# A gated mix of attention and feed-forward: the last gate factor applied earlier, and the last fill in two halves

## The chip, the cores and the metric

The kernel runs on one core of one Trainium2 chip. The metric is the device time of one execution in microseconds (us). In the profile PE is TensorE's matmuls, PEld its weight loads, DVE is VectorE, ACT ScalarE, POOL GpSimd and SP SyncE, which here only issues DMAs.

## The reference

With x of 2048 rows and 640 columns, out = g*a + (1-g)*b, where g = sigmoid(x . gate_w) is one number per row:

```python
g = _sigmoid((x * gate_w).sum(-1, keepdims=True))
a = _A_ref(x, A_wq, A_wk, A_wv, A_wo, A_beta)   # causal attention in 4 chunks of 512 rows, 32 heads of 20,
                                                # mixed with a running linear memory, then o @ wo
b = (silu(x @ w1) * (x @ w3)) @ w2              # feed-forward, 1728 inner columns
return g * a + (1 - g) * b
```

## The kernel before, in words

Everything is held transposed: 640 features are 5 blocks of 128 partitions, and the 2048 rows are 4 chunks (c = 0 to 3) of 512 columns. Chunks are worked in pairs, A = (0, 1) and B = (2, 3). Every fp32 factor of a large matmul is split into a high and a low part and multiplied in three passes (`PASSES`: high x high, weight's low x high, weight's high x low), so one projection of a block of 128 outputs over 640 inputs is 15 matmuls of 128x128 weights against 512 columns (`proj`).

The 1728 inner columns of the feed-forward are 14 units j (13 of 128, and j = 13 of 64), in five groups, the last of which is `[13, 12]`. `ffn_up(cs, j, ...)` computes for each chunk the gate product `pg`, then with ScalarE's tanh `t` and VectorE `u = (t+1)*pg`, then the product `pu`, then `t = u*0.5*pu`, and splits it into `ht` (high part by ScalarE, low part by GpSimd, line 107). For j = 13 gate and up products come out of one set of 15 matmuls, in the lower and the upper 64 partitions. `ffn_down(cs, js, ...)` multiplies the units of a group by w2: for each chunk and each of 5 feature blocks fb one PSUM bank, a fill, which VectorE adds to the sums `accs[c]`. The attention's output projection `oproj(c, ...)` adds to the same sums: its first part, `normalize`, divides the head outputs by their sums, adds the memory's read and splits the result; its second part is 5 fills of 15 matmuls (line 784), each added by VectorE.

The factor 1-g of a chunk, `shares[c]`, is one number per row, stored in DRAM and loaded by `load_share(c)` over all partitions (256 KB, from ScalarE's queue). (The attention's part is scaled by g/(1-g) in advance.) Chunk 0 gets it in its last down fills, chunk 1 in its output projection, and chunks 2 and 3 in their last down fills: `finish` adds the fill to the sum (line 515), multiplies by the share (line 516, by VectorE or, for even fb, by GpSimd) and stores the block from SP's queue (line 517). The very last block is added, multiplied and stored in two halves of 256 columns.

Weights come through `w_load` (SP's queue, into one of two raw buffers) and `w_split`: GpSimd casts the tile to its high part (line 174) and subtracts for the low part (line 175) into one of six W tiles; a raw buffer is free again after the low part, and a W tile after TensorE's last use. `w_get` asks for a tile; `w_step`, called at every step of the program that yields no float, loads and splits ahead.

PSUM banks (`bank_tile`) are taken in turn from a list of eight.

TensorE's order is the program's own: generators yield after a few matmuls, and `chain`, `braid` and `weave` mix them (`braid(a, b, every)` takes a step of b after each `every` steps of a). The order on the other engines is set by a planner with modelled costs, except where `here` keeps the program's order; each engine then works off its own list in that order. The end of the program, after the attention, is `tail`: the down fills of group 3, then units 13 and 12 for chunks 2 and 3, braided with `normalize(3)`; then the output projection of chunk 3; then the last down fills, 10 of them with 5 matmuls each.

## Time and profile before

| | us |
|---|---|
| three runs | 1109.91, 1107.6, 1111.63 (median 1109.91) |
| the profiled execution | 1109.41 |
| its span, first to last instruction | 1107.7 |
| PE busy | 1094.4 (99%) |
| DVE, POOL, ACT busy | 592.6 (53%), 584.7 (53%), 381.2 (34%) |

The profile is of one execution. A row of a timeline has the start, the duration, engine, line, operation, what is written and read with its shape, and in brackets the engine's idle time before it and who ended it. A row marked x2 or more merges neighbours: the duration is from the first start to the last end. SPq and ACTq rows are the issue of a DMA alone. The ends of matmuls are modelled. The granted TensorE clock is 1.000 of full speed.

### The profile page before, as it was taken

How to read it: one execution, taken by the hardware profiler on the slowest of the kernel's cores; microseconds unless marked ns; L12 is line 12 of the kernel's file. 1: busy time of each engine (PE TensorE's matmuls, PEld its weight loads, DVE VectorE, ACT ScalarE, POOL GpSimd, SP SyncE). 2: the span in 40 equal slices, each digit the busy share in tenths (PEclk: the TensorE clock that was granted, in tenths of full speed). 3: DMA queues.
4: the chain of work that ended last, by engine and by line, in shares of the span. 5: the costliest groups of instructions: out<-in, count | busy, mean ns of one | idle time of the engine just before them, and what ended most of it. 6: DMA issues, size and time to landing. Idle time of an engine off the chain costs nothing.

```text
span 1107.7 us, 17867 instructions
## 1 busy us (share of the span) xinstructions
PE 1094.4 (99%) x6285; PEld 852.9 (77%) x6285; DVE 592.6 (53%) x1708; ACT 381.2 (34%) x826; POOL 584.7 (53%) x729
## 2 busy tenths in 40 slices
PE   9999999999999999999999999999999999999997
PEld 6988877777777777788977777777777777777786
DVE  5032564356555554366154678875557765551645
ACT  6244233343233122145244543424343332233120
POOL 5055556366366363565175547555764556565253
PEclk9999999999999999999999999999999999999999
DMA  9266943334165132636268967455654433432122
GB/s 327 89 205 220 282 123 82 95 82 125 46 165 127 53 82 93 156 95 196 95 203 269 288 203 193 104 156 144 162 136 113 108 96 94 113 103 87 51 79 95
DMA packets 87545, 153.20 MB, mean 138 GB/s; under 512 B 11584, under 2 KB 25184, under 8 KB 87456
## 3 DMA queue, kind: packets, MB, share of 16 engines
q1 hardware_dynamic: 63040, 106.30, 30.4%
q0 software_dynamic: 20384, 38.68, 15.8%
q10 hardware_dynamic: 4032, 7.08, 1.8%
q8 instruction: 50, 0.82, 0.3%
q14 instruction: 39, 0.32, 0.1%
HBM read 96.56 MB, written 54.54 MB: 136 GB/s over the span
## 4 chain that ended last, share of the span: by engine, by line
PE 91%; DVE 4%; DMA 1%; ACT 1%; issue 1%; POOL 1%; SPq 0%; ACTq 0%; DVEq 0%; POOLq 0%
PE f L534 16%; PE g L253 16%; PE u L253 15%; PE v L364 6%; PE k L253 6%; PE op L784 6%; PE o L634 6%; PE q L253 6%; PE s L581 5%; PE t L614 4%; PE nd L331 1%; PE pm L428 1%; DVE junk L588 1%; PE pkt L413 1%; PE gt L713 1%
## 5 line engine op out<-in xcount | busy, mean ns | idle before, releaser
L588 DVE CUSTOM_DVE_ANT_0 junk<-s,mask 128x256 bf16<-128x256 f32 (+3 forms) x512 | 250.5, 489 | 106.3 <-PE s L581 74.1
L620 ACT ACTIVATE P<-t 128x512 f32<-128x512 f32 (+1 forms) x384 | 172.5, 536 | 192.1 <-PE t L614 154.8
L253 PE MATMUL g<-X,W 128*128 128x512 f32 x840 | 208.7, 398 | 0.0
L175 POOL TENSOR_TENSOR W<-wr,W 128x640 fp32r<-128x640 f32 (+1 forms) x126 | 200.3, 1596 | 2.3
L174 POOL CAST W<-wr 128x640 fp32r<-128x640 f32 (+1 forms) x126 | 91.0, 726 | 207.5 <-PE f L534 46.9
L534 PE MATMUL f<-ht,W 128*128 128x512 f32 x820 | 196.6, 397 | 0.3 <-POOL W L175 0.3
L253 PE MATMUL u<-X,W 128*128 128x512 f32 x780 | 196.7, 399 | 0.0
L624 POOL TENSOR_SCALAR_AFFINE_SELECT P<-P 128x256 f32<-128x256 f32 x192 | 94.6, 501 | 180.8 <-ACT P L620 180.6
L253 PEld LDWEIGHTS g<-X,W 128*128 128x128 f32 x840 | 155.9, 188 | 36.7 <-issue 0.4
L534 PEld LDWEIGHTS f<-ht,W 128*128 128x128 f32 x820 | 152.7, 188 | 37.0 <-POOL W L175 0.8
L253 PEld LDWEIGHTS u<-X,W 128*128 128x128 f32 x780 | 144.0, 188 | 34.5 <-ACT P L620 0.3
L107 POOL TENSOR_TENSOR ht<-ft,ht 128x512 fp32r<-128x512 f32 x52 | 67.1, 1291 | 91.3 <-ACT ht L106 90.8
L558 POOL DMA_DIRECT2D qk<-qkd x128 | 83.5, 654 | 0.3
L581 PE MATMUL s<-qk 60*128 60x256 f32 (+3 forms) x512 | 78.2, 345 | 2.2 <-DVE m L588 1.0
L253 PE MATMUL k<-X,W 128*128 128x512 f32 x300 | 77.0, 403 | 0.0
L634 PE MATMUL o<-P,vg 128*32 128x512 f32 (+3 forms) x1024 | 75.5, 435 | 1.4 <-DVE on L714 1.4
L253 PE MATMUL q<-X,W 128*128 128x512 f32 x300 | 74.0, 400 | 1.3 <-DVE X L107 0.7
L493 ACT ACTIVATE ft<-g 128x512 f32<-128x512 f32 x52 | 31.2, 599 | 125.7 <-PE g L253 114.7
L494 DVE SCALAR_TENSOR_TENSOR fu<-ft,g 128x512 f32<-128x512 f32 x52 | 35.7, 686 | 68.1 <-ACT ft L493 59.1
L364 PE MATMUL v<-W,X 128*128 128x320 f32 (+1 forms) x480 | 71.6, 311 | 0.3 <-ACT P L620 0.3
L364 PEld LDWEIGHTS v<-W,X 128*128 128x128 f32 x480 | 71.0, 189 | 0.8 <-ACT P L620 0.6
L106 ACT CAST ht<-ft 128x512 fp32r<-128x512 f32 x52 | 32.2, 619 | 111.9 <-DVE ft L500 111.8
(118 smaller groups left out, 1170.1 us busy)
## 6 DMA issues: line engine op xcount, KB each, us to landing
qk<-qkd POOLq DMA_DIRECT2D x128, 240.0 KB, 4.2
wr<-in_w_dram SPq DMA_DIRECT2D x80, 320.0 KB
qkd<-qs SPq DMA_DIRECT2D x20, 512.0 KB
qkd<-ks SPq DMA_DIRECT2D x20, 512.0 KB
od<-oq SPq DMA_DIRECT2D x32, 256.0 KB
wr<-in_wo_dram SPq DMA_DIRECT2D x20, 320.0 KB
vg<-vd SPq DMA_DIRECT2D x16, 336.0 KB
xr<-in_xT_dram SPq DMA_DIRECT2D x20, 256.0 KB
```

Source lines behind the costliest of these rows:

```text
L107: (lo or nc.gpsimd.tensor_sub)(dst[:, 1], src, dst[:, 0].bitcast(F32))
L174: nc.gpsimd.tensor_copy(w[:, 0, :n], raw[:, :n])
L175: nc.gpsimd.tensor_sub(w[:, 1, :n], raw[:, :n], w[:, 0, :n].bitcast(F32))
L253: nc.tensor.matmul(ps, w[:, a, kb * P:(kb + 1) * P], x[:, b, kb, :], start=n == 0, stop=n == 14)
L364: nc.tensor.matmul(ps[:, :n1 - n0], x[:, a, kb, lb * P:(lb + 1) * P], wvt[kb][:, b, n0:n1], start=n == 0, stop=n == 14)
L534: nc.tensor.matmul(ps, w, h, start=n == 0, stop=n == len(ms) - 1)
L558: here(nc.gpsimd.dma_start(t[64 * i:64 * i + RH], qkd[c][RH * (h + i):RH * (h + i + 1)]))
L581: nc.tensor.matmul(ps[i][:, o:o + w], q[:, qb * P:(qb + 1) * P], key[:, :w], start=n == 0, stop=n == len(todo) - 1, skip_group_check=True)
L588: nc.vector.tensor_tensor_reduce(out=junk[:, :w], in0=ps[i][:, o:o + w], in1=mask[:, L - w:], scale=1.0, scalar=-3.0e38, op0=ALU.add, op1= ...
L620: last["exp"] = nc.scalar.activation(pairs[2 * m + k]["P"][:, i, o:o + n], ps[i][:, b:b + n], AF.Exp, scale=SCALE)
L624: nc.gpsimd.affine_select(d, d, pattern=[[0, 2], [0, n], [1, P]], base=0, channel_multiplier=-1, compare_op=ALU.is_ge, fill=0.0)
L634: nc.tensor.matmul(ps[32 * i:32 * i + 32, kb * P:], heads[2 * p + i]["v"][:, kb], pairs[p + i // 2]["P"][:, i % 2, o:o + n], start=kb == 0 ...
```

## The change

For chunks 2 and 3 the factor 1-g no longer comes behind the last fills. It goes into the addends instead:

- `ffn_up` for the units of the last group multiplies `u` by the share (VectorE), so the last fills come out scaled.
- The sums so far are scaled before the last fills: those of chunk 3 right after the output projection's add, by VectorE; those of chunk 2 by GpSimd, in five steps braided into the output projection of chunk 3 (`shared(2)`).
- The last fills are then only added and stored (`finish_shared`).
- The two shares are loaded after the down fills of group 3 (`both_shares`), ahead of units 13 and 12; that of chunk 3 takes the slot of the head outputs `oq` in place of one of the four `f` tiles.
- The last fill of chunk 3 is made in two halves of 256 columns, each in a bank of its own.

The new generators add seven steps to the program, so `normalize`'s last step is braided 6 matmuls earlier, ahead of unit 13, and `w_step` is called seven times more.

```diff
     def ffn_up(cs, j, idx, oldest=None):
         half = j == NF
+        shares_in = cs == B and j in GROUPS[-1]
...
                 nc.vector.scalar_tensor_tensor(u, t, 1.0, pg, op0=ALU.add, op1=ALU.mult)
+                if shares_in:
+                    nc.vector.tensor_mul(u, u, shares[c])
...
                 nc.vector.scalar_tensor_tensor(u[:64], t[:64], 1.0, pg[:64], op0=ALU.add, op1=ALU.mult)
+                if shares_in:
+                    nc.vector.tensor_mul(u[:64], u[:64], shares[c][:64])
...
-    def finish(c, fb, ps, end=False):
-        dst = accs[c][:, fb]
-        for n0 in ((0, 256) if end else (0,)):
-            d, p, g = (t[:, n0:n0 + (256 if end else L)] for t in (dst, ps, shares[c]))
-            nc.vector.tensor_add(d, p, d)
-            (nc.gpsimd if c and fb % 2 == 0 and not end else nc.vector).tensor_mul(d, d, g)
-            nc.sync.dma_start(out[c, fb, :, n0:n0 + d.shape[-1]], d)
+    def share(c, fb):
+        d = accs[c][:, fb]
+        (nc.gpsimd if c == 2 or c == 1 and fb % 2 == 0 else nc.vector).tensor_mul(d, d, shares[c])
+
+    def finish(c, fb, ps):
+        d = accs[c][:, fb]
+        nc.vector.tensor_add(d, ps, d)
+        share(c, fb)
+        nc.sync.dma_start(out[c, fb], d)
+
+    def finish_shared(c, fb, ps, n0, n):
+        d = accs[c][:, fb, n0:n0 + n]
+        nc.vector.tensor_add(d, ps[:, :n], d)
+        nc.sync.dma_start(out[c, fb, :, n0:n0 + n], d)
+
+    def shared(c):
+        for fb in range(KB):
+            share(c, fb)
+            yield 1
...
-            if c in last:
+            if c in last and c < 2:
                 load_share(c)
...
+                for n0, n1 in ((0, 256), (256, L)) if last and (c, fb) == (NSEG - 1, KB - 1) else ((0, L),):
...
+                        nc.tensor.matmul(ps[:, :n1 - n0], w, h, start=n == 0, stop=n == len(ms) - 1)
...
+                    elif c < 2:
+                        finish(c, fb, ps)
+                    else:
+                        finish_shared(c, fb, ps, n0, n1 - n0)
+    def both_shares():
+        for c in B:
+            load_share(c)
+            yield 1
...
-        shares[c] = f_tile("sh") if c == NSEG - 1 else sp.tile([P, L], F32, tag="share", name=f"sh{c}", bufs=1)
+        shares[c] = sp.tile([P, L], F32, tag="oq" if c == NSEG - 1 else "share", name=f"sh{c}", bufs=1)
...
                     nc.vector.tensor_add(dst, ps, dst)
+                    if c == NSEG - 1:
+                        share(c, fb)
...
-    tail = [braid(chain([d] + u), o1, 4, 10)] + [o2, job_down(B, 4, B)]
+    tail = [braid(chain([d, (0, both_shares())] + u), o1, 4, 10)] + [braid(o2, (0, shared(2)), 3), job_down(B, 4, B)]
```

The planner's order on GpSimd for the end of the program, before and after (wo1 to wo5 are the output projection's weight tiles in their order of use, w2h and w2 those of units 13 and 12, "ht" the low part of unit 12, x share the multiplies by the share):

```
before: cast wo1, cast wo2, low wo1, low wo2, cast wo3, cast wo4, low wo3, low wo4, ht chunk 2,
        cast wo5, low wo5, cast w2h, ht chunk 3, low w2h, cast w2, low w2, 5 x share (chunks 2 and 3)
after:  cast wo1, cast wo2, low wo1, 5 x share (chunk 2), low wo2, cast wo3, cast wo4, low wo3, ht chunk 2,
        low wo4, cast wo5, ht chunk 3, cast w2h, low wo5, low w2h, cast w2, low w2
```

On TensorE, VectorE, ScalarE and SP the orders of the two kernels are alike up to `normalize(3)`, apart from names.

More of the change, by code (lines that the diff above doesn't have):

```diff
@@ L527, in ffn_down @@
             for fb in range(KB):
-                ps = bank_tile(f"f{c}_{js[0]}_{fb}", 1300 if len(js) > 2 else 690)
-                ms = []
-                for j, w in zip(js, w2s):
-                    for a, b in (PASSES if j < NF else ((0, 0), (0, 1))):
-                        ms.append((w[:, b, fb * P:(fb + 1) * P], hts[c, j][:, a, :]))
-                for n, (w, h) in enumerate(ms):
-                    nc.tensor.matmul(ps, w, h, start=n == 0, stop=n == len(ms) - 1)
-                    if n % 3 == 2 and n < len(ms) - 1:
-                        yield 699.0 if n == 2 and len(ms) > 5 else 699
-                filled()
-                dst = accs[c][:, fb]
-                if first:
-                    nc.scalar.copy(dst, ps)
-                elif c not in last:
-                    nc.vector.tensor_add(dst, ps, dst)
-                else:
-                    finish(c, fb, ps, (c, fb) == (NSEG - 1, KB - 1))
-                yield 699 if len(ms) % 3 == 0 else 466
+                for n0, n1 in ((0, 256), (256, L)) if last and (c, fb) == (NSEG - 1, KB - 1) else ((0, L),):
+                    ps = bank_tile(f"f{c}_{js[0]}_{fb}_{n0}", 1300 if len(js) > 2 else 690)
+                    ms = []
+                    for j, w in zip(js, w2s):
+                        for a, b in (PASSES if j < NF else ((0, 0), (0, 1))):
+                            ms.append((w[:, b, fb * P:(fb + 1) * P], hts[c, j][:, a, n0:n1]))
+                    for n, (w, h) in enumerate(ms):
+                        nc.tensor.matmul(ps[:, :n1 - n0], w, h, start=n == 0, stop=n == len(ms) - 1)
+                        if n % 3 == 2 and n < len(ms) - 1:
+                            yield 699.0 if n == 2 and len(ms) > 5 else 699
+                    filled()
+                    dst = accs[c][:, fb]
+                    if first:
+                        nc.scalar.copy(dst, ps)
+                    elif c not in last:
+                        nc.vector.tensor_add(dst, ps, dst)
+                    elif c < 2:
+                        finish(c, fb, ps)
+                    else:
+                        finish_shared(c, fb, ps, n0, n1 - n0)
+                    yield 699 if len(ms) % 3 == 0 else 466
+    def both_shares():
+        for c in B:
+            load_share(c)
+            yield 1
     oall, heads, pairs = {}, {}, {}
```

## The prediction

> **What bounds the kernel now.** The page comes first, then the chain of waits over the last 40 us, then the timelines of that stretch engine by engine.

> ```profile
> PE 1094.4 (99%) x6285; PEld 852.9 (77%) x6285; DVE 592.6 (53%) x1708; ACT 381.2 (34%) x826; POOL 584.7 (53%) x729
> ```

> TensorE (PE) is busy 99% of the span, 1094.4 of 1107.7 us. Time can be won where it has nothing more to do, and is lost wherever it is made to wait. The instruction streams of the two kernels as built differ in this last stretch alone (normalize of chunk 3, units 13 and 12, the output projection of chunk 3, last fill), so the sum concerns these 60 us. The chain there:

> ```profile
> 1069.50 3.50 PE u L253 x15
> 1073.00 17.50 PE op L784 x75
> 1090.50 8.08 PE f L534 x35
> ...
> 1101.83 1.27 DVE acc L516
> 1103.10 0.67 DVE acc L515 x2
> 1103.77 0.33 DVE acc L516
> 1104.10 0.34 DVEq L1020
> ```

> TensorE carries it through 75 matmuls of the projection (17.50/75 = 0.233 each) into the last fills; then VectorE takes over. The timelines of the end:

> ```profile
> 1090.34 11.70 PE L534 MATMUL f<-ht,W 128*128 128x512 f32 x50
> ...
> 1093.57 0.73 DVE L516 TENSOR_TENSOR acc<-acc,sh 128x512 f32<-128x512 f32 x1
> ...
> 1101.28 1.28 POOL L516 TENSOR_TENSOR acc<-acc,sh 128x512 f32<-128x512 f32 x1 [1.23 <-DVE acc L515]
> 1101.83 1.27 DVE L516 TENSOR_TENSOR acc<-acc,sh 128x512 f32<-128x512 f32 x1
> 1103.02 0.74 DVE L515 TENSOR_TENSOR acc<-f,acc 128x256 f32<-128x256 f32 x2
> 1103.69 0.74 DVE L516 TENSOR_TENSOR acc<-acc,sh 128x256 f32<-128x256 f32 x2
> 1104.13 0.83 SPq L517 DMA_DIRECT2D out_dram<-acc  x2
> ```

> TensorE ends at 1090.34 + 11.70 = 1102.04. VectorE is behind: its multiply at 1101.83 takes 1.27 where that at 1093.57 took 0.73, since it stands until GpSimd's own multiply ends at 1102.56. Two adds and two multiplies of 256 columns follow, to 1103.69 + 0.74 = 1104.43. From there to the span's end at 1107.7 are 3.25 us (last stores issued, landed, closing): a tail that remains.

> **Part 1, the end of the tail.** In the changed kernel the last ten fills are followed by an add alone, and the last fill comes as two halves in banks of their own. VectorE then needs 0.69 of each 1.17 us fill and can't fall behind.

> ```profile
> L515 DVE TENSOR_TENSOR acc<-f,acc x16: 408/684/693, 498.0 to 1103.4; 128x512 f32<-128x512 f32 x14, 128x256 f32<-128x256 f32 x2
> ```

> After TensorE's end stands one add of 256 columns: 1102.04 + 0.02 + 0.41 = 1102.47 instead of 1104.43, a gain of **1.96**. The output stores come out evenly, one per fill, instead of in pairs; I leave the 3.25 us behind the last VectorE instruction as they are, give or take 0.3.

> **Part 2, ten matmuls of 256 columns for five of 512.** No row has 256 columns against 128x128 weights. The nearest:

> ```profile
> 546.75 2.54 PE L364 MATMUL v<-W,X 128*128 128x320 f32 x16
> ```

> At most 2.54/16 = 0.159 each for 320 columns; at least half of 0.233, 0.117, for 256. So 10 x 0.117 to 0.159 less 5 x 0.233: 0.0 to +0.43. The rows at 512 and 320 columns make the cost nearly proportional to columns, so I take **+0.05**.

> **Part 3, multiplies that move under TensorE.** Units 13 and 12 get one multiply per chunk, four of up to 0.69 on VectorE; unit 12's stands behind u's 15 matmuls (3.50 us in the chain above), and unit 13's product isn't read until the last fills, 25 us later. Chunk 3's five multiplies come after the projection's adds, which are 3.5 us apart with 2.81 idle:

> ```profile
> 1026.40 0.33 SPq L640 DMA_DIRECT2D od<-oq  x1
> ...
> 1090.54 0.69 DVE L795 TENSOR_TENSOR acc<-op,acc 128x512 f32<-128x512 f32 x1 [2.81 <-PE op L784]
> 1091.68 0.69 DVE L515 TENSOR_TENSOR acc<-f,acc 128x512 f32<-128x512 f32 x1 [0.45 <-PE f L534]
> ```

> The fifth runs to about 1091.9 and delays the first fill's add (1091.68) by 0.2, which the next fill's slack takes up. The two share loads move ahead in ScalarE's queue, before its last copy for normalize; chunk 3's now uses the slot of the head outputs, whose last store was issued at 1026.40, so it waits for nothing. All this costs nothing as long as VectorE has these gaps; if its cover went, the five multiplies would cost at most 5 x 0.69 = 3.4. The five multiplies of chunk 2 are another matter.

> **Part 4, GpSimd's queue.** GpSimd splits each weight tile (a cast, then the low part), makes ht's low part, and runs strictly in its order. Before:

> ```profile
> 1051.52 2.04 POOL L175 TENSOR_TENSOR W<-wr,W 128x640 fp32r<-128x640 f32 x1
> ...
> 1056.52 0.93 POOL L174 CAST W<-wr 128x640 fp32r<-128x640 f32 x1 [0.99 <-DMA wr<-in_wo_dram]
> ...
> 1069.57 0.72 POOL L174 CAST W<-wr 128x640 fp32r<-128x640 f32 x1 [0.77 <-PE g L253]
> 1070.37 1.57 POOL L175 TENSOR_TENSOR W<-wr,W 128x640 fp32r<-128x640 f32 x1
> 1073.07 0.72 POOL L174 CAST W<-wr 128x640 fp32r<-128x640 f32 x1 [1.13 <-PE u L253]
> 1074.45 1.30 POOL L107 TENSOR_TENSOR ht<-ft,ht 128x512 fp32r<-128x512 f32 x1 [0.67 <-ACT ht L106]
> ```

> The pair at 1069.57 and 1070.37 is the projection's fifth and last weight tile, ready at 1071.94. In the changed stream the five multiplies of chunk 2 stand after the first tile's low part (the row at 1051.52), ahead of the second tile's low part, and all behind them moves. The fifth tile's cast and low part are no longer neighbours: between them come ht's low part for unit 12 of chunk 3 and the cast of the next tile (w2h). ht's low part cannot start before 1074.45, since it waits for ScalarE and that for TensorE's u, which ends at 1073.00. So the fifth tile's low part is ready at the earliest at 1074.45 + 1.30 + 0.72 + 1.57 = **1078.0**. When does TensorE want it?

> ```profile
> 1075.40 0.42 PEld L784 LDWEIGHTS op<-gm,W 128*128 128x128 f32 x2
> 1075.63 0.63 PE L784 MATMUL op<-gm,W 128*128 128x512 f32 x2
> ```

> These are the 13th and 14th matmuls of the projection, the fifth tile's high and low part; the low part's weight load starts at 1075.40 + 0.23 = 1075.63. TensorE, which also runs in order, stands for at least 1078.0 - 1075.6 = **2.4 us**.

> Does the chain before add to this? The share's load, then:

> ```profile
> 1051.56 0.62 ACT L715 CAST gm<-on 128x512 fp32r<-128x512 f32 x1 [0.77 <-DVE on L714]
> 1053.58 0.34 SPq L163 DMA_DIRECT2D wr<-in_wo_dram  x1
> ...
> 497.50 0.32 ACTq L687 DMA_DIRECT2D sh<-ed  x1
> 502.03 0.69 DVE L516 TENSOR_TENSOR acc<-acc,sh 128x512 f32<-128x512 f32 x1 [1.44 <-DMA sh<-ed]
> ```

> The load follows the copy of 1051.56. A weight load of the same microseconds is used 1056.52 - 1053.58 = 2.94 after its issue, a share amid other traffic 502.03 - 497.50 = 4.53: the first multiply starts at 1054.5 (at most 1056.1). I take 2.94, as the queues are as quiet there. Five multiplies of 1.30, plus 0.45 for each that meets a VectorE instruction with both inputs in SBUF (the low part of a tile took 2.04 at 1051.52, 1.57 at 1070.37). VectorE has nine such by the code up to unit 12's first product; with four met, 5 x 1.30 + 4 x 0.45 = 8.3: 1062.8. The second tile's low part, 2.04, ends at 1064.8; only then is its raw buffer free and SP issues the fourth tile's load, 2.94: 1067.8. Cast 0.72, third tile's low part 1.57, ht of chunk 2 1.30, fourth tile's low part 2.04: 1073.4. Now SP issues w2h's load, 2.94: 1076.4; its cast 0.72, the fifth tile's low part 1.57: 1078.7, a wait of 3.1. With no meetings and a load 0.6 us quicker the floor of 2.4 binds; I take **2.7**. With every value at its upper end (4.53; 1.75, 2.04, 0.93 throughout) the same walk ends at 1082.5: 6.9 us.

> The row that prices a meeting is 2.04 against 1.57, 0.47 more. [...]

> After the stall all of TensorE's work, the last tile's cast that waits for it, and the last fills are shifted alike. SP's queue has only stores left behind the late loads.

> **Sum.** -1.96 + 0.05 + 2.7 = **+0.8 us**. The profiled execution took 1109.41 (span 1107.7, 1.7 around it): 1110.2. The median of the three runs shown, 1109.91, lies 0.5 above it, so as a median **1110.7**. 0.3%, about what a measurement of this kernel can tell from no change, is 3.3 us.

> **Rivals.** (a) The tail's gain alone: GpSimd's late tile doesn't hold TensorE. For it: GpSimd idles much here, and the stall rests on one inversion in its order. Against it: a tile ready at 1071.94 has 3.7 us of slack, and ht, one cast and one low part alone use 6.1. It gives 1109.91 - 1.9 = 1108.0. (b) The load queue decides: a share that lands as late as at 497.50 and meetings all along, so that the fourth and w2h tiles come late one after the other; stall 6.9, sum +5.0, 1114.9: slower. It passes 0.3% when the stall passes 3.3 + 1.9 = 5.2, that is when the walk above is 2.1 us later than I reckon. For it: the load of 4.53. Against it: that one was issued amid x and weight loads. (c) The change doesn't shorten the tail: if the stores' landing, not VectorE, sets the end, only half of 1.96 is won; sum +1.8, 1111.7. Against it: the last store is issued right behind the last multiply, at 1104.55.

> **How the numbers follow.** Forecast (stall 2.4 to 3.5, tail won) 0.58; (a) 0.15; (b) 0.17; (c) 0.10. The likeliest: 1110.7, its own range 1109.5 to 1112. Runs of the kernel before lie 1107.6 to 1111.63 apart, so the range takes in (a) and a good part of (b): 1107.3 to 1114.0. Over 0.3% faster: only scatter on top of (a), 0.08. Over 0.3% slower: most of (b) and scatter, 0.2. Within: 0.72.

> **What would show it.** Right: in the projection's first fill TensorE waits 2.4 to 3.5 us for GpSimd's W low part, just behind ht's low part and a cast; the five multiplies of chunk 2 lie between about 1054 and 1063; VectorE's last add ends 0.43 after TensorE's end, and the span 3.25 later. Wrong: no wait of TensorE in the projection (then (a)); a second wait there, on the fourth tile (then (b)); a longer stretch than 3.3 us behind the last add (then (c)); or a wait of TensorE elsewhere.

## The result, and the profile after

| | before | changed |
|---|---|---|
| median of 20 runs each, us | 1110.05 | 1112.51 |
| lowest and highest | 1107.53, 1113.42 | 1109.53, 1116.02 |
| profiled execution, us | 1109.41 | 1111.28 |
| its span | 1107.7 | 1109.4 |

The ratio is 1.0020, with a 95% interval of 1.0011 to 1.0028: 2.2 us slower (1.2 to 3.1), within the 0.3% that was called no change. The forecast was 1110.7 as a median (+0.8), range 1107.3 to 1114.0. The range holds 1112.51; the narrower 1109.5 to 1112, which the prediction gave for its likeliest outcome, does not.

The chain that ended last, in the profile of the changed kernel (start, duration, engine and what it writes, line):

```profile
1050.56 3.46 DMA sh<-ed
...
1054.16 2.21 POOL acc L518 x2
...
1057.12 5.14 POOL acc L518 x3
1062.26 2.00 POOL W L175
...
1064.27 2.78 DMA wr<-in_wo_dram
...
1070.68 1.99 POOL W L175
...
1072.69 2.86 DMA wr<-in_w2h_dram
...
1075.68 0.72 POOL W L174
1076.39 1.50 POOL W L175
...
1077.93 16.26 PE op L810 x62
1094.19 11.55 PE f L553 x55
...
1105.77 0.42 DVE acc L529
```

Before, this stretch of the chain was TensorE's alone, then VectorE's. Now 27 us of it go through the share's load, GpSimd's five multiplies and the weight tiles behind them; TensorE comes back for 62 of the projection's 75 matmuls. VectorE has one add of 256 columns at the end and nothing else.

The timeline of TensorE at that place:

```profile
1074.62 0.39 PE L810 MATMUL op<-gm,W 128*128 128x512 f32 x1
1077.93 0.80 PE L810 MATMUL op<-gm,W 128*128 128x512 f32 x1 [2.92 <-POOL W L175]
1078.53 0.63 PE L810 MATMUL op<-oall,W 128*128 128x512 f32 x1
1078.96 0.63 PE L810 MATMUL op<-gm,W 128*128 128x512 f32 x1
```

TensorE stands 2.92 us before the 14th matmul, for the low part of the fifth weight tile. But look at the rows behind the wait: the matmuls start 0.43 apart (1078.53, 1078.96), not 0.233. The windows of busy time (length, busy time of PE, PEld, DVE, ACT, POOL, then the granted clock) say why:

```profile
1074.48:1077.89 3.41, 0.53 (x3) 0.09 (x1) 0.00 (x0) 0.00 (x0) 2.47 (x4) 1.00 0.13 52
1077.89:1081.30 3.41, 3.37 (x8) 2.70 (x9) 1.38 (x2) 0.00 (x0) 1.50 (x1) 0.50 0.33 96
1081.30:1084.71 3.41, 3.41 (x16) 2.73 (x16) 0.95 (x2) 0.00 (x0) 0.00 (x0) 1.00 0.00 0
```

In the 3.41 us that follow the stretch with the wait, the granted clock is 0.50, and eight matmuls are in the row where sixteen are in the next. This cost is in no step of the prediction.

In this profile the whole end of the program lies about 1 us earlier than in the profile before: the projection's first matmul starts at 1071.82 against 1072.83. Profiles of kernels below differ as much there (1071.81 in e2_order, 1073.51 in e1_late). So the two spans differ by 1.7 us only, although more is lost from there on, and times of the two profiles have to be compared as distances.

### The profile page after: what moved, and what is told of

Its sections match the earlier page's. It is cut to its first block, busy times and chain, and to the rows that moved or that the text cites. A ratio compares the mean times of both kernels' runs of the same rounds, so it can differ in the third digit from the quotient of the medians.

```text
span 1109.4 us, 17888 instructions
## 1 busy us (share of the span) xinstructions
PE 1096.5 (99%) x6290; PEld 855.3 (77%) x6290; DVE 597.6 (54%) x1711; ACT 381.2 (34%) x826; POOL 585.3 (53%) x729
## 4 chain that ended last, share of the span: by engine, by line
PE 90%; DVE 3%; POOL 2%; DMA 2%; issue 1%; ACT 1%; SPq 0%; ACTq 0%; DVEq 0%; POOLq 0%
PE f L553 16%; PE g L253 15%; PE u L253 15%; PE v L364 6%; PE k L253 6%; PE o L660 6%; PE op L810 6%; PE q L253 6%; PE s L607 5%; PE t L640 4%; PE nd L331 1%; PE pm L428 1%; POOL W L175 1%; DVE junk L614 1%; POOL acc L518 1%
## 5 line engine op out<-in xcount | busy, mean ns | idle before, releaser
L253 PE MATMUL g<-X,W 128*128 128x512 f32 x840 | 208.5, 398 | 0.0
L174 POOL CAST W<-wr 128x640 fp32r<-128x640 f32 (+1 forms) x126 | 91.5, 730 | 211.8 <-PE f L553 50.0
L175 POOL TENSOR_TENSOR W<-wr,W 128x640 fp32r<-128x640 f32 (+1 forms) x126 | 199.7, 1590 | 2.2
L253 PE MATMUL u<-X,W 128*128 128x512 f32 x780 | 196.8, 399 | 0.0
L553 PE MATMUL f<-ht,W 128*128 128x512 f32 (+1 forms) x825 | 196.6, 395 | 0.2 <-POOL W L175 0.2
L253 PEld LDWEIGHTS g<-X,W 128*128 128x128 f32 x840 | 156.0, 188 | 36.5 <-issue 0.4
L253 PEld LDWEIGHTS u<-X,W 128*128 128x128 f32 x780 | 144.1, 188 | 34.4 <-ACT P L646 0.3
L107 POOL TENSOR_TENSOR ht<-ft,ht 128x512 fp32r<-128x512 f32 x52 | 67.0, 1289 | 86.1 <-ACT ht L106 85.9
L253 PE MATMUL k<-X,W 128*128 128x512 f32 x300 | 77.1, 404 | 0.0
L253 PE MATMUL q<-X,W 128*128 128x512 f32 x300 | 74.2, 401 | 0.9 <-DVE X L107 0.7
L364 PE MATMUL v<-W,X 128*128 128x320 f32 (+1 forms) x480 | 71.6, 311 | 0.3 <-ACT P L646 0.3
L364 PEld LDWEIGHTS v<-W,X 128*128 128x128 f32 x480 | 71.0, 189 | 0.8 <-ACT P L646 0.6
L106 ACT CAST ht<-ft 128x512 fp32r<-128x512 f32 x52 | 32.2, 619 | 111.2 <-DVE ft L503 111.1
```

What stands on the lines that cost most here:

```text
L107: (lo or nc.gpsimd.tensor_sub)(dst[:, 1], src, dst[:, 0].bitcast(F32))
L174: nc.gpsimd.tensor_copy(w[:, 0, :n], raw[:, :n])
L175: nc.gpsimd.tensor_sub(w[:, 1, :n], raw[:, :n], w[:, 0, :n].bitcast(F32))
L253: nc.tensor.matmul(ps, w[:, a, kb * P:(kb + 1) * P], x[:, b, kb, :], start=n == 0, stop=n == 14)
L364: nc.tensor.matmul(ps[:, :n1 - n0], x[:, a, kb, lb * P:(lb + 1) * P], wvt[kb][:, b, n0:n1], start=n == 0, stop=n == 14)
L553: nc.tensor.matmul(ps[:, :n1 - n0], w, h, start=n == 0, stop=n == len(ms) - 1)
```

## The experiments

The theory that the experiments test: the halves and the earlier factor win what was forecast at the end (about 2 us); the inversion in GpSimd's list (the last two tiles' low parts and ht behind five multiplies) makes TensorE wait; and the wait costs more than its own length, since the clock is halved behind it. Rivals: the multiplies themselves cost time by contention; the gain at the end is not won in full; the extra 1.5 us lie somewhere else.

**The five multiplies, later on GpSimd (e1_late).** They keep their engine, but stand behind the last weight tiles:

```diff
-        (nc.gpsimd if c == 2 or c == 1 and fb % 2 == 0 else nc.vector).tensor_mul(d, d, shares[c])
+        m = (nc.gpsimd if c == 2 or c == 1 and fb % 2 == 0 else nc.vector).tensor_mul(d, d, shares[c])
+        if c == 2:
+            here(m)
```

> The changed kernel, with chunk 2's five multiplies still on GpSimd but kept behind all weight splits that stand ahead of them in the program, so that they run beside the output projection. Theory A (the five multiplies ahead of the weight tiles make TensorE wait 3 us for the fifth tile, and the halved clock after that wait costs 1.7 more; the tail's gain is 2.0): no wait of TensorE for W in the projection, granted clock 1.00 there, the end of the tail as in the changed kernel; 2.0 us faster than before, ratio 0.998, and 4.7 us faster than the changed kernel. Rival B (the loss comes from VectorE's nine added multiplies or from the earlier share loads): no faster than the changed kernel, ratio 1.002. Rival C (the tail's gain does not show in the time): ratio 1.000.

Measured: 1107.9, ratio 0.9984 (0.9976 to 0.9993). In its timeline the multiplies lie under the projection, and in its chain TensorE carries all 75 matmuls without a wait:

```profile
1076.38 1.58 POOL L175 TENSOR_TENSOR W<-wr,W 128x640 fp32r<-128x640 f32 x1
1077.91 7.20 POOL L518 TENSOR_TENSOR acc<-acc,sh 128x512 f32<-128x512 f32 x5
```

```profile
1073.67 17.50 PE op L812 x75
...
1102.75 0.42 DVE acc L531
```

The gain at the end is there (1.8 us by the ratio, 1.96 forecast) once the place of the multiplies is changed. They still run on GpSimd, now beside the projection, and their contention costs nothing there that can be seen: the 75 matmuls take 17.50 us, as in the kernel before.

**The same multiplies on VectorE (e4_vec).**

```diff
-        (nc.gpsimd if c == 2 or c == 1 and fb % 2 == 0 else nc.vector).tensor_mul(d, d, shares[c])
+        (nc.gpsimd if c == 1 and fb % 2 == 0 else nc.vector).tensor_mul(d, d, shares[c])
```

> The changed kernel, with chunk 2's five multiplies on VectorE instead of GpSimd. Theory A: GpSimd's order of tiles is that of before again, the fifth tile is ready before TensorE wants it, no wait; ratio 0.998. Rival B: VectorE has five more multiplies, so at least as slow as the changed kernel, ratio 1.002 or more.

Measured: 1107.08, ratio 0.9978 (0.9968 to 0.9988). No wait of TensorE in the projection. This one and e1_late are both faster than the kernel before and, by their ratios to it, than the changed one; between the two the intervals overlap. Both keep the earlier share loads and VectorE's nine added multiplies, so the loss does not come from these.

**Early multiplies, but no inversion (e2_order).** The multiplies stay where the change put them; only the list behind them is kept so that the fifth tile's low part comes ahead of ht and of the next cast:

```diff
+            m = nc.gpsimd.tensor_copy(w[:, 0, :n], raw[:, :n])
+            if k >= len(items) - 3 > 100:
+                here(m)
...
-                split(ht, t)
+                split(ht, t, lo=(lambda *x: here(nc.gpsimd.tensor_sub(*x))) if (c, j) == (NSEG - 1, 12) else None)
```

> The changed kernel, with chunk 2's five multiplies early on GpSimd as they are, but the fifth tile's low part kept ahead of ht's low part of chunk 3 and of w2h's cast. If the swap of these decides, as the prediction had it: the fourth tile's low part ends 2.0 us ahead of the time at which TensorE wants the fifth's, cast and low part take 2.3, so TensorE waits 0.3 us or not at all, the clock stays 1.00, ratio 0.998 to 0.999. If the late loads behind the multiplies decide whatever the order: a wait of 2 us or more stays, ratio 1.000 to 1.002.

Measured: 1107.47, ratio 0.9987 (0.9978 to 0.9995). GpSimd's timeline, and TensorE's 13th and 14th matmul:

```profile
1054.00 8.11 POOL L520 TENSOR_TENSOR acc<-acc,sh 128x512 f32<-128x512 f32 x5 [1.45 <-DMA sh<-ed]
...
1070.35 2.02 POOL L177 TENSOR_TENSOR W<-wr,W 128x640 fp32r<-128x640 f32 x1
1072.32 0.72 POOL L174 CAST W<-wr 128x640 fp32r<-128x640 f32 x1
1073.12 1.58 POOL L177 TENSOR_TENSOR W<-wr,W 128x640 fp32r<-128x640 f32 x1
1074.65 1.30 POOL L506 TENSOR_TENSOR ht<-ft,ht 128x512 fp32r<-128x512 f32 x1
```

```profile
1074.61 0.64 PE L812 MATMUL op<-gm,W 128*128 128x512 f32 x2
```

The multiplies take the same 8.1 us at the same place and the fourth tile is nearly as late as in the changed kernel (low part from 1070.35 here, 1070.62 there). But the fifth tile's low part ends at 1074.70, 3.2 us earlier than 1077.89, and no wait of TensorE is left in the projection. So the delay alone cost nothing, if by a hair: the 14th matmul, due at 1074.61 + 0.23 = 1074.84, had its tile ready for 0.14 us. The edit moves two things behind the fifth tile, ht's low part and the w2h cast. In the changed kernel ht's ends at 1074.73, and the cast stands until its load lands (2.86 in the chain): the load came last there.

**The end of the tail, part by part (e3_whole, e5_halves).** e3_whole is e1_late with the last fill whole; e5_halves is the kernel before with the last fill in two halves and the factor still behind the fills. The line that makes e3_whole's fill whole:

```diff
-                for n0, n1 in ((0, 256), (256, L)) if last and (c, fb) == (NSEG - 1, KB - 1) else ((0, L),):
+                for n0, n1 in ((0, L),):
```

> The kernel with late multiplies on GpSimd, but the last fill whole: one bank, one add of 512 columns, one store of 256 KB. It tells the two halves' own worth. Theory: behind TensorE's end an add of 0.69 in place of 0.42 and a store twice as large: 0.3 to 0.6 us more behind TensorE's end, and TensorE 0.0 us shorter; ratio to before 0.9985 to 0.999. If the halves carry the tail's gain: 1.5 us or more lost, ratio 1.000.

> The kernel before with the last fill in two halves alone, shares still applied behind the fills. Theory: VectorE is behind by a multiply that waits for GpSimd, so the halves bring little: 0 to 0.4 us, ratio 0.9997 to 1.000. If the halves carry the gain: 1.5 us or more, ratio 0.9985.

Measured: e3_whole 1107.45, ratio 0.9983 (0.9974 to 0.9991); e5_halves 1109.34, ratio 0.9998 (0.9989 to 1.0007). The chains, e3_whole first, then e5_halves:

```profile
1090.41 11.55 PE f L555 x50
...
1101.98 0.69 DVE acc L531
```

```profile
1098.14 1.27 DVE acc L514
1099.42 1.53 DVE acc L513 x3
1100.95 0.99 DVE acc L514
```

With the fill whole, TensorE ends at 1101.96 and the span at 1105.6, 3.64 us later. With halves (the changed kernel) it is 1105.74 to 1109.4, 3.66. The last add takes 0.69 instead of 0.42, yet no time is lost, and halves alone leave VectorE behind with its multiplies as before. So the whole gain is that of the factor that moved; the halves are worth nothing that these runs can show.

**Waits of a set length in the kernel before (e6_hold4, e6_hold6b, e6_hold9b).** Does the cost belong to the wait, whatever makes it? GpSimd gets a fill and 4, 6 or 9 multiplies on a spare tile ahead of the fifth tile's low part, with ht and the next cast behind it:

```diff
+            if k == len(items) - 2 > 100:
+                here(m)
+            if k == len(items) - 3 > 100:
+                z = sp.tile([P, L], F32, tag="share", name="z", bufs=1)
+                here(nc.gpsimd.memset(z, 1.0))
+                for _ in range(4):
+                    here(nc.gpsimd.tensor_mul(z, z, z))
+                here(nc.gpsimd.tensor_sub(w[:, 1, :n], raw[:, :n], w[:, 0, :n].bitcast(F32)))
+                return
...
-                split(ht, t)
+                split(ht, t, lo=(lambda *x: here(nc.gpsimd.tensor_sub(*x))) if (c, j) == (NSEG - 1, 12) else None)
```

> The kernel before, with a fill and four multiplies of 128x512 on a spare tile put on GpSimd ahead of the fifth tile's low part, and the two instructions behind it kept behind it: a wait alone, with nothing else of the change. The tile is ready about 5.5 us later, 3.7 of which are slack: TensorE waits 1.5 to 2 us. If a wait costs what it lasts: +1.5 to 2 us, ratio 1.0015. If every wait over a microsecond also halves the clock for 3.4 us: +3.3 to 3.7, ratio 1.003. Theory A says that the clock drops only after a longer wait: 1.00 here.

> The kernel before with the wait alone, now six multiplies on a spare tile ahead of the fifth tile's low part (four gave a wait of 0.8 us at 1.10 each): a wait of 3.0 us, as long as that of the changed kernel. Theory A: the wait and, where the clock's window falls into it, 1.7 us of halved clock behind it, 3.0 to 4.7 us in all, ratio 1.0027 to 1.0042, which is the changed kernel's loss without its tail gain of 2.0. Rival (a wait costs what it lasts): clock 1.00, ratio 1.0027.

> The same with nine: a wait of 6.3 us, longer than one window of 3.4 us of the clock's steps. Theory A: the clock drops in every execution, by one window or two; 6.3 + 1.7 = 8.0 us or more, ratio 1.0072. Rival (a wait costs what it lasts): 6.3 us, ratio 1.0057, clock 1.00 behind the wait.

TensorE's wait (line waited at, releaser, total, times, longest) and, from the chain, the 62 matmuls behind it, for 4, 6 and 9 multiplies in this order:

```profile
PE op L793 <- POOL W L182: 0.8, 1, 0.8
...
1079.33 14.73 PE op L793 x62
```

```profile
PE op L793 <- POOL W L182: 3.0, 1, 3.0
...
1082.21 16.28 PE op L793 x62
```

```profile
PE op L793 <- POOL W L182: 6.3, 1, 6.3
...
1083.45 17.31 PE op L793 x62
```

| | wait | 62 matmuls behind it | worked out | measured ratio | in us |
|---|---|---|---|---|---|
| 4 | 0.8 | 14.73 | 0.8 + 0.3 = 1.1 | 1.0007 (0.9998 to 1.0017) | 0.8 |
| 6 | 3.0 | 16.28 | 3.0 + 1.8 = 4.8 | 1.0038 (1.0026 to 1.0050) | 4.2 |
| 9 | 6.3 | 17.31 | 6.3 + 2.8 = 9.1 | 1.0085 (1.0072 to 1.0099) | 9.4 |

62 matmuls at 0.233 are 14.47, so 0.3, 1.8 and 2.8 us are lost behind the wait on top of it. (The wait with 4 came out at 0.8 us where 1.5 to 2 were expected, since a multiply on a tile with itself took 1.10, not 1.30.) The wait and the matmuls are from one profile each, the ratio from all runs. For 9, the record has the clock at 0.50 for two stretches on end:

```profile
1075.49:1078.91 3.42, 1.61 (x7) 0.96 (x6) 0.00 (x0) 0.00 (x0) 3.19 (x4) 1.00 0.00 0
1078.91:1082.32 3.41, 0.00 (x0) 0.00 (x0) 0.00 (x0) 0.00 (x0) 3.25 (x4) 1.00 0.00 0
1082.32:1085.73 3.41, 2.28 (x5) 1.82 (x6) 0.69 (x1) 0.00 (x0) 3.33 (x4) 0.50 0.67 186
1085.73:1089.15 3.42, 3.42 (x9) 2.64 (x8) 0.00 (x0) 0.00 (x0) 1.19 (x1) 0.50 0.16 63
```

With 4 the clock behind the wait stays 1.00. So a wait in this place has a price of its own: nearly its length when it is short, 1.8 us above it at 3 us, 2.8 at 6.3. With 9 the times alone say so too: the rival, a wait that costs what it lasts, gives 1.0057, below the interval. With 6 its 1.0027 lies just inside, and there the trace decides.

**The changed kernel twice more (e7_again1, e7_again2).** Is the halved clock there each time?

> The changed kernel once more, for a second look at the clock. Theory A with windows that run free of the program: the wait for the fifth tile is 2.9 us again, and the clock behind it is halved for 3.4 us or not at all, depending on where the windows lie: projection 21.4 us (halved, as in the first profile) or 19.7 to 20.6. If the drop belongs to every such wait: halved again.

> The same, a third look: wait of 2.9 us, clock behind it halved or not.

Measured: 1110.49 and 1111.63 (one run each). The waits and the windows around them, e7_again1 first:

```profile
PE op L810 <- POOL W L175: 2.6, 1, 2.6
...
1074.63:1078.04 3.41, 0.91 (x4) 0.77 (x5) 0.14 (x1) 0.00 (x0) 3.17 (x3) 1.00 0.00 0
1078.04:1081.45 3.41, 3.41 (x10) 2.63 (x9) 1.24 (x2) 0.00 (x0) 0.56 (x1) 0.50 0.33 96
```

```profile
PE op L810 <- POOL W L175: 2.5, 1, 2.5
...
1078.97:1082.38 3.41, 3.41 (x10) 2.62 (x9) 1.39 (x2) 0.00 (x0) 0.72 (x1) 0.50 0.35 96
```

In all three profiles one stretch of 3.41 us is halved behind the wait, although TensorE was not idle for the whole of the stretch ahead of it (0.53, 0.91 and 0.91 us busy). The halved stretch does not begin with the work behind the wait: it starts 0.04 us ahead of the 14th matmul in the first profile (1077.89 against 1077.93), 0.91 and 0.73 us behind it in the two others (1078.04 against 1077.13, 1078.97 against 1078.24). In the first profile the clock is halved once more behind the end of TensorE's work: from 1108.61, which is 27.31 us, eight times 3.41, behind the end of the other halved stretch, and with TensorE busy for 0.53 of the 3.41 us ahead of it.

How little work a stretch has when the next one is halved can be narrowed down from the rows of all thirteen profiles, with stretches counted in steps of 3.41 us from a halved one. Over their last 40 us, a stretch at full clock with TensorE busy for up to 1.12 us of 3.41 was followed by a halved one in every case, and one with 1.61 or more in none. The wait of 6.3 us shows the upper figure: it begins in the row of 1075.49 above, with 1.61 us busy, and the next stretch is still at 1.00. The lower one is the end of TensorE's work in e1_late:

```profile
1101.59:1105.00 3.41, 1.12 (x10) 0.92 (x8) 1.44 (x3) 0.00 (x0) 0.00 (x0) 1.00 0.62 231
1105.00:1106.40 1.40, 0.00 (x0) 0.00 (x0) 0.00 (x0) 0.00 (x0) 0.00 (x0) 0.50 0.00 0
```

The mean clock of each of the 20 runs points the same way without a profile (3.41 us at half are 0.15% of the mean): 11 runs of the changed kernel had 0.998, 7 had 0.997, and two 1.000. Those two took 1109.53 and 1110.32; the 11 took 1112.2 on average, the 7 took 1113.8. (The two may be waits that fell across two stretches; that is not shown.) It is a hint, since the mean also counts a stretch halved at the program's start or behind TensorE's end: of the 33 runs of the kernel before that go with e1_late, 5 had 0.998 or less without any such wait.

**The wait filled with idle matmuls (e8_keep).** If the clock makes the difference, it must go when TensorE has something to do during the wait:

```diff
+                        if (c, fb, kb, b) == (NSEG - 1, 0, KB - 1, 0) and a == 0:
+                            spin = bank_tile("spin")
+                            for i in range(9):
+                                here(nc.tensor.matmul(spin, ws[0][:, 0, :P], oT[0][:, 0], start=i == 0, stop=i == 8))
```

> The changed kernel with nine matmuls more (128x512, into a bank that nobody reads) put on TensorE's queue between the first fill's thirteenth matmul and the one that waits for the last weight tile's low part. Nine at 0.233 us are 2.1 us, less than the 2.5 to 2.9 us that TensorE waited there in the three profiles of the changed kernel, so the wait should shrink to 0.4 to 0.8 us and the matmul that waits should start at the same time after GpSimd's subtraction as before. Theory with the clock: the 3.41 us at a granted clock of 0.5 that stood behind the wait in all three profiles don't come, the 75 matmuls of the projection are 0.233 us apart from the wait on, and the time is 1.7 us under the changed kernel's: ratio to the kernel before 1.0020 - 0.0015 = 1.0005, within 1.000 to 1.001. Rival, the clock is not set by TensorE's idleness there (it halves all the same), or the 1.7 us lie elsewhere: ratio 1.002, as the changed kernel itself, or above it by what of the nine outlasts the wait.

Measured: 1111.43, ratio 1.0012 (1.0002 to 1.0023). TensorE's timeline, and the 62 matmuls in its chain:

```profile
1077.11 2.26 PE L815 MATMUL spin<-gm,W 128*128 128x512 f32 x9
1079.66 0.50 PE L810 MATMUL op<-gm,W 128*128 128x512 f32 x1 [0.29 <-POOL W L175]
```

```profile
1079.66 14.74 PE op L810 x62
```

GpSimd is as late as before (its low part ends at 1079.61, TensorE had no other work from 1077.11), but the 62 matmuls take 14.74 instead of 16.26 to 16.28, and 8 of 12 runs have a mean clock of 1.000. By the trace the clock's share is 1.5 us, and this part is shown. By the times the kernel lies 0.8 thousandths below the changed one, where 1.5 were expected: 1.0012 is outside the 1.000 to 1.001 that was named, and its interval takes in both theories' numbers. The times alone do not settle it. (The profiled execution's own mean is 0.998, but its granted clock is 1.00 from 1074 to 1109, so what is missing lies ahead of the projection.)

## Why the prediction was right, and what it left out

**Part 1, the end of the tail: right.** VectorE's last instruction ends at 1106.19, 0.45 after TensorE's (0.43 forecast), and the span 3.2 later (3.25). From TensorE's end to the span's it is 3.66 us, 5.66 before: 2.0 won, 1.96 forecast. The four kernels without the wait (e1_late, e2_order, e3_whole, e4_vec) lie 1.4 to 2.4 us below the kernel before. The step "one add of 256 columns" was right in the timeline and of no consequence: e3_whole ends as early with 512.

**Part 2, ten matmuls for five: +0.05, right.** 55 matmuls take 11.55 where e3_whole's 50 take 11.55.

**Part 3, multiplies under TensorE: costless, right.** e4_vec adds five more of them to VectorE, and is no slower.

**Part 4, GpSimd's queue: right in its mechanism, and nearly in its steps.** The walk had the fifth tile ready at 1078.7, 3.1 us after TensorE wants it. The trace has 1077.89, with TensorE wanting it at 1074.62 + 0.23 = 1074.85, so 3.04. The two profiles are 1 us apart, so the steps compare from the copy that the share's load follows (1051.56 before, 1050.56 in the changed kernel): the walk has the first multiply 2.9 later and the tile 27.1 later, the trace 3.6 and 27.3. The share's load took 3.46 (2.94 taken, 4.53 the bound), and the later steps made up most of that. The five multiplies took 8.1 (8.3 reckoned, with 0.45 for each of four that meet a VectorE instruction): the first took 1.29 and the other four 1.74. That speaks for the 0.47 of the row: 1.74 is 0.45 more than 1.29. VectorE paid as well: its instruction that met the first took 1.60 in place of 0.69. What came last was the w2h tile's load, as the walk had it. The stall of 2.7 was 2.9, 2.6 and 2.5 in three profiles. (The upper end of 6.9 takes 4.53 for the share's load alone; with 4.53 for the two weight loads as well the walk would end 3.2 us later.)

**The sum: a term was missing.** It priced a wait of TensorE at its own length, and that is the one step that fell short. Behind this wait the restart costs 0.3 (14.73 for 62 matmuls with no halved clock, against 14.47) and the halved clock 1.5 (16.26 against 14.73). With them the sum is -1.96 + 0.0 + 2.9 + 1.8 = +2.7 for the profiled execution, and 2.3 to 2.4 for the other two; measured were +2.2 by the ratio (1.2 to 3.1) and +2.46 by the medians. The two profiled spans fit as well: 2.7 less the 1.0 by which the changed kernel's projection started earlier is the 1.7 between them. The two of the 20 runs whose clock stayed at 1.000 are at -0.5 and +0.3 against the median before, near the forecast of +0.8. The call of no change held because its limit, 3.3 us, had room for the 1.8 us left out; that much was luck.

**The rivals.** (a) is out: the wait is there. (c) is out: the tail is won in full. (b) did not happen, but its price was too low for the same reason: a wait of 6.3 us cost 9.4, so 0.3% would have been passed well before the stall of 5.2 that (b) named, at about 3.3 + 1.96 - 1.8 = 3.5 us (an estimate).

What stays open is the exact bound on a stretch's idle time, between 1.8 and 2.3 us by the rows. Waits of 2.5 us and more halved the clock in all five profiles that have one, one of 0.8 did not; nothing between was tried.

## What to carry to other kernels

Work that is moved to an engine with slack is not priced by its duration but by the order it leaves behind: here five multiplies of 8 us were harmless under TensorE, and ahead of the weight tiles too, by a margin of 0.14 us, as long as the tile that was needed first stayed first in the list (ratios 0.9984 and 0.9987 against 1.0020). Where TensorE is the bound, price a wait that takes some 2 us or more (the estimate above) out of one 3.41-us stretch with the halved clock behind it, 1.5 us in this kernel, not by its length alone, and look at the granted clock in windows of 3.4 us; the mean over the span (0.998) hides it.

## What the runs showed of the hardware

The halved stretches behind the waits are 3.41 us long in the rows above, and within that of the changed kernel matmuls of 512 columns are 0.427 apart against 0.233, so one costs 1.5 us (16.26 against 14.73 for the 62 matmuls) and not a full half of 3.41. One of the same length lies at a program's start: in the profile of e6_hold4 the clock is halved from 8.11 to 11.52, while the first loads come in, and its span is 1111.2 with a wait of only 0.8:

```profile
4.70:8.11 3.41, 2.25 (x7) 0.84 (x6) 1.72 (x3) 1.88 (x4) 0.67 (x1) 1.00 0.90 322
8.11:11.52 3.41, 3.27 (x7) 1.99 (x8) 3.17 (x5) 3.08 (x6) 1.09 (x2) 0.50 1.05 401
```

TensorE was busy for 2.25 us of the stretch ahead of it, more than the 1.61 that did no harm at the end of the program, so busy time alone does not explain the start. The profiles of the kernel before and of the changed kernel have none there: their granted clock is 1.00 over the first 20 us. Such a stretch comes and goes without any change at that end of the program, and may be part of the scatter of these runs (1107.53 to 1113.42 before); that was not separated.
